# Linear attention beside an MLP on one core: the pass order of the key sums in six tiles, two relus and an operand split issued ahead of the values' products, and w2's first split issued behind a copy

## The chip, the cores and the metric

One core of a Trainium2 chip runs the whole kernel. The metric is the device time of one execution in microseconds. Of the kernel before there are three timed runs and one profiled execution, whose trace is read below.

The engines by their names in the trace: PE is TensorE (its matmuls), PEld its weight loads, DVE is VectorE, ACT is ScalarE, POOL is GpSimd, SP issues transfers. Each engine works through its own instructions in the order in which the program lists them, and waits for the others through semaphores. All times are in microseconds.

## The reference

The input is x (2048 tokens of 512 numbers), normalised to xn. Two branches read xn and their results are added to x:

```python
def attention(xn, wqkv, wo):                 # 32 heads of 16
    q, k, v = split_heads(xn @ wqkv)
    phi = lambda t: where(t > 0, t + 1, exp(t)) + 1e-6
    kv  = einsum("bhsd,bhse->bhde", phi(k), v)
    z   = einsum("bhsd->bhd", phi(k))
    num = einsum("bhqd,bhde->bhqe", phi(q), kv)
    den = einsum("bhqd,bhd->bhq", phi(q), z) + 1e-6
    return merge_heads(num / den) @ wo

def mlp(xn, w1, b1, w2, b2):                 # 512 -> 1376 -> 512
    r = relu(xn @ w1 + b1)
    return (r * r) @ w2 + b2

out = x + attention(layernorm(x), wqkv, wo) + mlp(layernorm(x), w1, b1, w2, b2)
```

## The kernel before

**Numbers in two parts.** Matmul operands are pairs of float32r tiles: a high part, which is the number rounded by a copy (mostly on ScalarE), and a low part, the number less its high part (a subtraction on VectorE or, for the tokens, on GpSimd). A product then is three matmuls: high by high, high by low, low by high. `split` (line 117) makes both parts.

**The order of work is written out by hand.** The program is recorded under a manual schedule: each engine gets its instructions in the order in which the Python code issues them, and semaphores are set by the tiles that the instructions share. Moving a line of Python therefore moves an instruction in the queue of its engine, and nothing else is rearranged.

**First stage: the tokens, tile by tile.** Sixteen tiles of 128 tokens are loaded, normalised and turned. The loop of line 778 runs over them. For tile i it projects the keys (`project`, line 367: twelve matmuls into a bank `pk`), makes phi of the keys (`phi`, line 359, on ScalarE and VectorE), then `parts` (line 373) gives phi's high part on ScalarE and its low part on VectorE (line 378), and `tokens` (line 349) makes the two parts of the normalised tokens of the next tile, the high part on ScalarE, the low part on GpSimd (line 119). Behind that, `kx` (line 384) adds tile i - 1 into four banks: the product of the tokens (turned) by phi(k). This is the key sum from which the attention's values are made later, since the weights of the values are applied after the sum. `kx` issues twelve matmuls in three groups of four. `tok[i][:, u]` with u = 0 or 1 is the high or low part of the tokens, `pk[i][:, v]` that of phi. For tiles 0 to 7 the groups come in the order (0,0), (0,1), (1,0): phi's low part is read by the second group, the tokens' low part by the third. Tiles 8 to 15 have an order of their own. A bank is done when all three groups are in, in whichever order.

**Work that is spread.** A list `extra` holds operand preparations for the next stage, each a small function; `more()` issues the next few of them at fixed places (the counts are written out on line 766).

**Between the stages** (lines 848 to 963, with n = 0). PE runs, in this order: `plain_1` into `pz` (twelve matmuls: the last, partly filled group of the MLP's hidden units, for the last 512 tokens), the last `kx`, `plain_1` into `pz2` (the same units for the 512 tokens before), and the values' products: `values()` (line 870) has 32 matmuls of 128 columns into a bank `pkv`; then VectorE masks the result to its heads (line 880, tile `kv`) and `split` makes its parts (tile `kvt`: the high part on ScalarE, the low part on VectorE). After `values()` one `more()` comes, then `relu` twice (line 475, ScalarE: the banks `pz` and `pz2` into `rz` and `r2[NF - 1]`, tiles `r2c`), then the remaining preparations of `extra`, then `piece_2(NF - 1, 0)` (line 196), which loads the last rows of w2 and returns two functions: one for the high part (ScalarE) with copies of it on GpSimd, and one for the low part (VectorE).

**Second stage** (line 1024). Queries and hidden units are made for two groups of 512 tokens at a time by a scheme that saves products: with weights and tokens cut into two halves each, seven products of six matmuls stand for eight. `product` (line 484) is one of them; its weights come from tiles `aop`, its tokens from the turned tokens `xs0`, `xs1` or from sums and differences `T[1]` to `T[4]`, and sums of weights are called S1 to S4. Every step p issues, with A, B and C as banks: A from A11; B from A12, adding c11, a copy of A in SBUF; C from S1 by T[1] and its copy t5; then more. In step 0 the small products `matrix(j)` (line 885, bank `pm`) stand between them; they read `kvt`. C's bank in step 0 is the one that held `pz`. `next_2(t)` (line 974) issues the functions that `piece_2` returned and asks for the next piece of w2; before the change it is called with 0 ahead of the loop, that is, ahead of step 0's products and copies, for both n. For n = 1 the list of pieces is empty at that point.

Accumulation of both branches, the residual and the store follow and are not touched.

Of the kernel before, what the change touches and what calls it, by code (L numbers as in the profile page):

```python
# [18 lines left out]
def kernel(  # L19
# [41 lines left out]
    NPE = 2 * TB  # L61
# [16 lines left out]
    def bank(name, tag="ps"):  # L78
        return psum.tile([P, 512], F32, name=name, tag=tag)

    def w512(name, tag, bufs):
        return work.tile([P, 512], F32, name=name, tag=tag, bufs=bufs)
# [26 lines left out]
    def copy(eng, o, i, bias=0.0):  # L109
        if eng == "act":  # L110
            nc.scalar.activation(o, i, AF.Copy, bias=bias)  # L111
        elif bias:
            ENG[eng].tensor_scalar(o, i, bias, None, op0=OP.add)
        else:
            ENG[eng].tensor_copy(o, i)

    def split(h, l, src, eh, el):
        copy(eh, h, src)
        ENG[el].tensor_tensor(out=l, in0=src, in1=f32(h), op=OP.subtract)  # L119
# [76 lines left out]
    def piece_2(f, at):  # L196

        h, l = w2s[f] = [w2r[at // 2][:, at % 2 * 2 + u] for u in range(2)]
        if f < NF - 1:
            t = raw(f"r2_{f}", w2[f * P:(f + 1) * P, :])  # L200
            return [lambda: copy("act", h, t), lambda: rest_of(l, t, h)]


        t = w512(f"r2_{f}", "raw", 6)
        for a, o, n in units(f):
            nc.sync.dma_start(t[a:a + n], w2[o:o + n, :])

        def high():
            copy("act", h, t)
            copy("pool", l[2 * Q:], h[:2 * Q])  # L210
            if "q" not in w2s:
                w2s["q"] = work.tile([P, D], F32R, name="w2q", tag="w2q")
                for k in range(TB):
                    copy("pool", w2s["q"][k * Q:(k + 1) * Q], h[2 * Q:3 * Q])

        def low():
            rest_of(l[:2 * Q], t[:2 * Q], h[:2 * Q])
            rest_of(h[3 * Q:], t[3 * Q:], h[3 * Q:])

        return [high, low]  # L220
# [161 lines left out]
        phi(ps, kp[i], mid, late)  # L382

    def kx(i):
        order = (((1, 0),), ((0, 0), (0, 1))) if i >= NPE else (((0, 0),), ((0, 1),), ((1, 0),))
        todo = [(c, u, v) for group in order for c in range(NJ) for u, v in group]
        first, last = order[0][0], order[-1][-1]
        for c, u, v in todo:
            nc.tensor.matmul(kxp[c], lhsT=tok[i][:, u, c * P:(c + 1) * P], rhs=pk[i][:, v],  # L389
                             start=i == 0 and (u, v) == first, stop=i == NT - 1 and (u, v) == last)  # L390
# [21 lines left out]
    def steps_of(t, j, done=False, parts=False):  # L412


        o = q[t][:, j]
        tiles = []
        blocks = lambda ap: ap.rearrange("p (r c) -> p r c", c=32)
        heads_of = lambda ap: ap.rearrange("p (h d) -> p h d", h=H)
        by_heads = lambda ap: ap.rearrange("p (r h) d -> p r h d", h=2)

        def weighted():
            pz = w512(f"pz{t}_{j}", "p", 6)
            tiles.append(pz)
            nc.scalar.activation(pz, o, AF.Identity, bias=zc[:, 1, j:j + 1], scale=zc[:, 0, j:j + 1])

        def sums():
            pt = w512(f"pt{t}_{j}", "p", 6)
            den = small.tile([P, H], F32, name=f"dt{t}_{j}", tag="den")
            nc.vector.transpose(blocks(pt), blocks(tiles[0]))
            nc.vector.tensor_reduce(den, heads_of(pt), axis=AX.X, op=OP.add)  # L430
            tiles.append(den)

        def quotients():
            pz, den = tiles
            nc.vector.tensor_scalar(den, den, 1e-6, None, op0=OP.add)
            nc.vector.reciprocal(den, den)
            nc.vector.transpose(by_heads(heads_of(pz)), by_heads(den[:, :, None].to_broadcast([P, H, D // H])))

        def divide():
            nc.vector.scalar_tensor_tensor(o, o, 1e-6, tiles[0], op0=OP.add, op1=OP.mult)  # L440

        def into_parts():
            a = aT[t, j] = places.pop(0)
            split(a[:, 0], a[:, 1], o, "act", "dve")

        return [lambda: phi_T(o, o)][done:] + [weighted, sums, quotients, divide] + [into_parts][:parts]
# [28 lines left out]
    def relu(o, i, f):  # L475
        nc.scalar.activation(o, i, AF.Relu, bias=b1s[:, f:f + 1])

    def plain_1(ps, w, x):

        for j in range(NJ):  # L480
            three(ps, [w[:, u, j * P:(j + 1) * P] for u in range(2)],
                  [x[u][:, j, :] for u in range(2)], j == 0, j == NJ - 1)

    def product(ps, a, b, first=False, last=False):

        for j in range(2):
            for n, (u, v) in enumerate(PASSES):
                nc.tensor.matmul(ps, lhsT=a[u][:, j * P:(j + 1) * P], rhs=b[v][:, j, :],  # L488
                                 start=first and j == 0 and n == 0, stop=last and j == 1 and n == 2,
                                 skip_group_check=True)  # L490
# [50 lines left out]
    for i0 in range(0, NT, TB):  # L541
# [5 lines left out]
        n = TB if i0 >= NPE else NPE - NDVE  # L547
        o = work.tile([P, n, 512], F32, name=f"xg{i0}", tag="r0" if i0 + TB == NT else "r3" if i0 >= NPE else "rc")
        for k in range(0, n, 2):
            i = i0 + TB - n + k  # L550
# [172 lines left out]
    def do(what, k=1):  # L723
        for _ in range(k):
            if what:
                what.pop(0)()
# [39 lines left out]
    extra, counts = [], [[0, 0, 0, 0, 0, 1, 1, 0, 0, 1, 2, 2, 0, 1, 4, 1, 2]]  # L766

    def more(i=None):

        if i is None or i > 12:  # L770
            do(extra, counts[0].pop(0))
# [3 lines left out]

    kxp = [bank(f"kx{c}", "acc") for c in range(NJ)]
    kx(0)
    for i in range(2, NT):
        if i == 3:
# [60 lines left out]
        if i in (3, 6):  # L840

            b = i // 6
            for u in range(2):
                nc.sync.dma_start(xsd[b][u], f32(cols(b * TB)[u]))
        kx(i - 1)
        more(i)

# [4 lines left out]
    plain_1(pz, z, xlast[0])  # L852
    more()
    kx(NT - 1)
    kxs = [two(f"kxs{c}") for c in range(2)]
    for c in range(NJ):
# [13 lines left out]
    def values():  # L870
        ps = bank("pkv", "acc")
        for c in range(NJ):
            for j in range(NJ):
                at = slice(j * P, (j + 1) * P)

                nc.tensor.matmul(ps[:, at], lhsT=wvs[:, c, at], rhs=kxs[c // 2][:, c % 2, at],  # L876
                                 start=c == 0 and j == 0, stop=c == NJ - 1 and j == NJ - 1,
                                 skip_group_check=True)
        t = w512("kv", "p", 6)
        nc.vector.tensor_tensor(out=t.rearrange("p (j d) -> p j d", j=NJ), in0=ps.rearrange("p (j d) -> p j d", j=NJ),  # L880
                                in1=heads[:, None, :].to_broadcast([P, NJ, P]), op=OP.mult)
        kvt[0] = work.tile([P, 2, 512], F32R, name="kvt", tag="r3")
        split(kvt[0][:, 0], kvt[0][:, 1], t, "act", "dve")
# [16 lines left out]
    for n in range(2):  # L900
# [4 lines left out]
        order = [("q", 0), ("w", 0), ("q", 1), *(("w", k) for k in range(1, NP))]  # L905
# [37 lines left out]
        if n == 0:  # L943

            more()
            pz2 = bank("pz0b")
            plain_1(pz2, z, x2)
            more()
            values()
            more()  # L950

            rz = r2[1]
            relu(rz, pz, NF - 1)
            relu(r2[NF - 1], pz2, NF - 1)
            do(extra, len(extra))
            w2next = piece_2(NF - 1, 0)
        else:
            w2next = []
            pz = bank(f"pz{n}", "acc")
            plain_1(pz, z, x1)  # L960
# [13 lines left out]
        def next_2(t):  # L974

            do(w2next, 2 - highs.pop(0))
            if t + 1 < NF and (n == 0 or t >= TB - 1):
                f = w2order[t + 1]
                w2next.extend(piece_2(f, place(f)))

        def high_2():
            do(w2next)
            highs[0] = 1

        highs = [0] * NF
        next_2(0)


        banks = [bank(f"b{n}_{k}") for k in range(4)]
# [29 lines left out]
        def step(k=1):  # L1019

            for _ in range(k):
                do(steps[t1] or steps[t2])

        for p in range(NO + 1):
# [24 lines left out]
            if kind:  # L1049
                c11 = w512(f"c11_{n}_{p}", "p", 6)  # L1050
                copy("act", c11, A)
                product(B, A12, [x[:, 2:] for x in x1], True, True)
                if kind == "w":
                    high_2()
                nc.vector.tensor_tensor(out=c11 if kind == "w" else q[t1][:, fa], in0=B, in1=c11, op=OP.add)
                if kind == "w":
                    relu(c11, c11, fa)
                else:
                    steps[t1] += steps_of(t1, fa, parts=True)
                step(at_p[0])  # L1060
# [261 lines left out]
```

## Time and profile before

| | us |
|---|---|
| median of 3 timed runs | 415.05 (414.95 to 415.22) |
| the profiled execution | 415.3 |
| its span, first to last instruction | 413.6 |
| PE busy | 408.6 |
| PEld busy | 336.9 |
| DVE busy | 314.5 |
| ACT busy | 270.2 |
| POOL busy | 50.0 |

The span is what the trace shows; the time of the execution has 1.7 around it. PE's busy time is modelled from pipelined matmuls, so a busy PE may still be waiting between two of them; the weight loads show the waits, and the chain of waits, which follows the work that ended last back through the program, shows how long each run of matmuls really took. A row of the timeline gives start, length, engine, line, operation, the tile that is written and those that are read, their sizes, a count, and in brackets how long the engine stood idle before it and what it then waited for. A line of the source can be that of a helper: line 111 is every copy on ScalarE, line 119 every subtraction in `split`.

### The profile page before, as it was taken

Reading aid. Unit: us, or ns where it says so; the run is one execution under the profiler, and the core shown is the slowest. Engines: PE = TensorE matmul, PEld = TensorE weight load, DVE = VectorE, ACT = ScalarE, POOL = GpSimd, SP = SyncE. Lnnn points to the kernel's source line nnn. Section 1 sums busy time; section 2 is a strip of 40 time slices with the busy share of each in tenths; the row PEclk is TensorE's granted clock in tenths of the full one; section 3 lists DMA queues with packets and bytes.
Section 4 is the critical chain, followed back from the end, with each engine's and each line's share of the span. In section 5 each row is a group of like instructions: output and inputs, shape, how many; then the busy total and the mean of one; then the engine's idle time right before and its main releaser. Section 6 shows DMA issues by size and latency. Waiting matters only on the chain.

```text
span 413.6 us, 5427 instructions
## 1 busy us (share of the span) xinstructions
PE 408.6 (99%) x1835; PEld 336.9 (81%) x1835; DVE 314.5 (76%) x584; ACT 270.2 (65%) x487; POOL 50.0 (12%) x70
## 2 busy tenths in 40 slices
PE   8999999999999999999999999999999999999996
PEld 7788888888888888888878888888888888878885
DVE  6895667797699898998439996468989685449843
ACT  5867767756668888789547731567588857737420
POOL 3241222230130000020000040100000200000310
PEclk9999999999999999999999999999999999999999
DMA  7789572710321312264267991411120871025602
GB/s 248 272 247 353 204 228 101 234 48 2 102 77 52 101 41 72 93 177 78 89 246 251 385 198 75 129 52 48 54 79 25 228 183 47 2 86 168 103 0 101
DMA packets 44925, 54.62 MB, mean 132 GB/s; under 512 B 7905, under 2 KB 29153, under 8 KB 43618
## 3 DMA queue, kind: packets, MB, share of 16 engines
q1 hardware_dynamic: 42594, 50.09, 37.1%
q0 software_dynamic: 2304, 4.20, 6.5%
q8 instruction: 14, 0.23, 0.2%
q14 instruction: 13, 0.11, 0.1%
HBM read 41.16 MB, written 13.11 MB: 131 GB/s over the span
## 4 chain that ended last, share of the span: by engine, by line
PE 97%; DMA 1%; ACT 0%; SPq 0%; DVE 0%; issue 0%
PE acc L130 37%; PE b L488 32%; PE kx L389 11%; PE pk L370 11%; PE acc L499 2%; PE pz L130 1%; DMA rk<-in_A_wqkv_dram 1%; PE pkv L876 1%; PE pm L130 1%; PE pz0b L130 1%; PE b L130 1%; PE pt L309 1%; PE acc L506 0%; SPq L159 0%; PE end L130 0%; ACT wkh L111 0%
## 5 line engine op out<-in xcount | busy, mean ns | idle before, releaser
L130 PE MATMUL acc<-w2r,s 128*128 128x512 f32 x477 | 112.9, 390 | 0.0
L130 PEld LDWEIGHTS acc<-w2r,s 128*128 128x128 f32 x477 | 89.4, 188 | 19.3 <-issue 0.7
L488 PE MATMUL b<-T,aop 128*128 128x512 f32 x336 | 83.9, 390 | 0.0
L488 PEld LDWEIGHTS b<-T,aop 128*128 128x128 f32 x336 | 62.8, 188 | 13.9 <-DVE aop L119 0.4
L389 PE MATMUL kx<-pk,tok 128*128 128x512 f32 x192 | 46.8, 392 | 0.0
L389 PEld LDWEIGHTS kx<-pk,tok 128*128 128x128 f32 x192 | 35.6, 188 | 8.0 <-DVE pk L378 0.6
L488 PE MATMUL b<-xs0h,aop 128*128 128x512 f32 x112 | 36.9, 390 | 0.0
L1005 POOL DMA_DIRECT2D res<-in_B_b_dram x16 | 14.1, 1099 | 182.4 <-DVE dt L430 64.1
L130 PE MATMUL acc<-mh,aTsr 128*128 128x512 f32 x112 | 35.6, 389 | 0.0
L119 POOL TENSOR_TENSOR tok<-xp,tok 128x512 fp32r<-128x512 f32 x16 | 22.3, 1393 | 55.1 <-ACT tok L111 55.1
L1013 DVE TENSOR_TENSOR res<-acc,res 128x512 f32<-128x512 f32 x16 | 11.0, 692 | 23.1 <-PE acc L130 18.5
L122 DVE TENSOR_TENSOR w2r<-r,w2r 128x512 fp32r<-128x512 f32 (+2 forms) x35 | 25.2, 721 | 0.1
L111 ACT ACTIVATE aop<-S 128x512 fp32r<-128x512 f32 x28 | 17.5, 624 | 11.1 <-DVE S L705 11.1
L130 PEld LDWEIGHTS acc<-mh,aTsr 128*128 128x128 f32 x112 | 21.0, 188 | 4.4
L488 PEld LDWEIGHTS b<-xs0h,aop 128*128 128x128 f32 x112 | 21.0, 188 | 4.3
L119 DVE TENSOR_TENSOR aop<-S,aop 128x512 fp32r<-128x512 f32 x28 | 19.5, 697 | 4.3 <-ACT aop L111 3.9
L119 DVE TENSOR_TENSOR s<-c,s 128x512 fp32r<-128x512 f32 x20 | 13.6, 689 | 11.0 <-ACT s L111 11.0
L130 PE MATMUL acc<-ml,aTsr 128*128 128x512 f32 x56 | 21.8, 389 | 0.0
L488 PE MATMUL b<-xs0l,aop 128*128 128x512 f32 x56 | 21.8, 389 | 0.0
L111 ACT ACTIVATE w2r<-r 128x512 fp32r<-128x512 f32 x32 | 19.6, 619 | 2.6 <-DMA out_dram<-res 2.0
L111 ACT ACTIVATE T<-Tf 128x512 fp32r<-128x512 f32 x16 | 9.5, 628 | 16.5 <-DVE Tf L648 16.4
L488 PE MATMUL b<-xs1h,aop 128*128 128x512 f32 x56 | 19.5, 389 | 0.0
(197 smaller groups left out, 770.0 us busy)
## 6 DMA issues: line engine op xcount, KB each, us to landing
r<-in_B_w_dram SPq DMA_DIRECT2D x49, 256.0 KB, 3.0
res<-in_A_x_dram SPq DMA_DIRECT2D x8, 512.0 KB, 4.7
res<-in_B_b_dram POOLq DMA_DIRECT2D x16, 256.0 KB, 5.7
out_dram<-res SPq DMA_DIRECT2D x15, 256.0 KB, 2.1
x<-in_A_x_dram SPq DMA_DIRECT2D x5, 512.0 KB, 5.8
via<-xp SPq DMA_DIRECT2D x5, 512.0 KB, 2.7
xg<-via SPq DMA_DIRECT2D x20, 128.0 KB, 2.9
xTd<-t SPq DMA_DIRECT2D x8, 256.0 KB, 3.4
```

The costliest lines, as they stand in the source:

```text
L111: nc.scalar.activation(o, i, AF.Copy, bias=bias)
L119: ENG[el].tensor_tensor(out=l, in0=src, in1=f32(h), op=OP.subtract)
L122: nc.vector.tensor_tensor(out=l, in0=src, in1=f32(h), op=OP.subtract)
L130: nc.tensor.matmul(ps, lhsT=a[u], rhs=b[v], start=first and n == 0, stop=last and n == 2)
L309: nc.tensor.transpose(t[k][:, at:at + P], xp[i][:, j * P:(j + 1) * P], ident)
L370: nc.tensor.matmul(ps, lhsT=cols(i)[u][:, j, slot(i)], rhs=w[v][:, j, :], start=first and n == 0, stop=last and n == len(steps) - 1)
L389: nc.tensor.matmul(kxp[c], lhsT=tok[i][:, u, c * P:(c + 1) * P], rhs=pk[i][:, v], start=i == 0 and (u, v) == first, stop=i == NT - 1 and ( ...
L488: nc.tensor.matmul(ps, lhsT=a[u][:, j * P:(j + 1) * P], rhs=b[v][:, j, :], start=first and j == 0 and n == 0, stop=last and j == 1 and n == 2,
L499: nc.tensor.matmul(ps, lhsT=s[u][:, k * P:(k + 1) * P], rhs=w2s[NF - 1][u][:, a:z], start=first and u == 0, stop=stop and u == 1)
L876: nc.tensor.matmul(ps[:, at], lhsT=wvs[:, c, at], rhs=kxs[c // 2][:, c % 2, at], start=c == 0 and j == 0, stop=c == NJ - 1 and j == NJ - 1 ...
L1005: nc.gpsimd.dma_start(r[:, i], b2[None, :].partition_broadcast(P), accum_op=OP.add)
L1013: nc.vector.tensor_tensor(out=r[:, a:z], in0=ps, in1=r[:, a:z], op=OP.add)
```

## The change

Three edits. In `kx`, tiles 2 to 7 get the order (0,0), (1,0), (0,1): the tokens' low part is read by the second group and phi's low part by the last; tiles 0 and 1 keep the old order, and so do 8 to 15. Between the stages the two relus and the next two entries of `extra` are issued ahead of `values()` instead of behind it, and the two `more()` around `values()` go; every entry of `extra` is still issued, once. The call `next_2(0)` ahead of the loop stays for n = 1; for n = 0 it moves into step 0, behind the copy c11.

```diff
     def kx(i):
-        order = (((1, 0),), ((0, 0), (0, 1))) if i >= NPE else (((0, 0),), ((0, 1),), ((1, 0),))
+        if i >= NPE:
+            order = ((1, 0),), ((0, 0), (0, 1))
+        elif i > 1:
+            order = ((0, 0),), ((1, 0),), ((0, 1),)
+        else:
+            order = ((0, 0),), ((0, 1),), ((1, 0),)
...
             pz2 = bank("pz0b")
             plain_1(pz2, z, x2)
             more()
-            values()
-            more()
 
             rz = r2[1]
             relu(rz, pz, NF - 1)
             relu(r2[NF - 1], pz2, NF - 1)
+            do(extra, 2)
+            values()
             do(extra, len(extra))
             w2next = piece_2(NF - 1, 0)
...
         highs = [0] * NF
-        next_2(0)
+        if n:
+            next_2(0)
...
                 c11 = w512(f"c11_{n}_{p}", "p", 6)
                 copy("act", c11, A)
+                if n == 0 and p == 0:
+                    next_2(0)
                 product(B, A12, [x[:, 2:] for x in x1], True, True)
```

Engine by engine, the program holds the same instructions in both versions. On PE only the two groups in `kx` of tiles 2 to 7 trade places, and the first and the third `pm` matmul now carry waits for `kvt`. ScalarE's order around the values' products was kvt, S1, relu, relu, part of A22, S3, w2, c11, t5; it is relu, relu, S1, kvt, the part of A22, S3, c11, w2, t5. VectorE's was kv, kvt, T[1]'s low part, S1's low part, T[2]'s; it is T[1]'s, S1's, kv, kvt, T[2]'s. The transfers and GpSimd's copies keep their order; the load of the next piece of w2 waits, before and after, for S1's low part, whose data held its buffer.

## The prediction

> **What bounds the kernel now.** I read the page first, then the waits of the weight loader (the half of TensorE where its waits show), then the chain of waits, then the timeline around each place where the chain takes longer than its matmuls need.
>
> ```profile
> span 413.6 us, 5427 instructions
> ...
> PE 97%; DMA 1%; ACT 0%; SPq 0%; DVE 0%; issue 0%
> ```
>
> The matrix engine is on the chain for 97% of the span, and the diff neither adds nor removes a matmul. So the change can only win what TensorE still waits, and only lose by making it wait anew. All of its waits that bear on the edits:
>
> ```profile
> PEld kx L389 <- DVE pk L378: 0.6, 2, 0.3
> PEld b L488 <- DVE aop L119: 0.4, 1, 0.4
> PEld b L488 <- ACT r2c L476: 0.3, 1, 0.3
> PEld b L488 <- DVE t L1037: 0.2, 1, 0.2
> ```
>
> These are idle times of the loader, part of which the matmul in flight hides. The chain (start, duration, what) shows what is really lost:
>
> ```profile
> 20.14 2.98 PE kx L389 x12
> ...
> 26.29 2.75 PE kx L389 x12
> ...
> 32.21 2.77 PE kx L389 x12
> ...
> 37.70 2.72 PE kx L389 x12
> ...
> 106.56 4.58 PE b L488 x18
> 111.14 1.39 PE pm L130 x6
> ...
> 125.26 9.64 PE b L488 x42
> ```
>
> Twelve undisturbed matmuls take 2.72, so one takes 0.227. Then 18 need 4.08 and lost 0.50 at 106.56; 42 need 9.52 and lost 0.12 at 125.26.
>
> **Part 1, the order of kx for tiles 2 to 7.** It swaps the second and third groups of four matmuls: tokens' low part with phi's high part now comes second, phi's low part third. The two waits for phi's low part (0.3 each) belong to tiles 0 and 1: their kx is the one that starts before 26 (the second is the 2.98 row), and these keep the old order. Tiles 4 to 7 run at 2.72 already, tiles 2 and 3 at 2.75 and 2.77 with no wait named. So at most 0.03 + 0.05 = 0.08 could be won. What can be lost: the tokens' low part is subtracted by GpSimd and is wanted four matmuls sooner. For tile 2 that is close:
>
> ```profile
> 24.69 1.96 POOL L119 TENSOR_TENSOR tok<-xp,tok 128x512 fp32r<-128x512 f32 x1 [4.25 <-ACT tok L111]
> ...
> L119 POOL TENSOR_TENSOR tok<-xp,tok 128x512 fp32r<-128x512 f32 x8 | 11.1, 1398 | 25.8 <-ACT tok L111 25.8
> ...
> 26.83 0.19 PEld L389 LDWEIGHTS kx<-pk,tok 128*128 128x128 f32 x1
> ```
>
> The subtraction ends at 24.69 + 1.96 = 26.65, and the fifth weight load of tile 2, which the new order feeds from it, starts at 26.83: 0.18 to spare. From tile 3 on the tokens are made a whole tile ahead: all eight subtractions of tiles 2 to 9 take 11.1, so the seven others 1.31 each, and tile 3's, next in the queue, is done near 28.0, four before its kx at 32.21. Nothing ahead of 26.83 is edited, so I take 0, with bounds of -0.08 and, should this subtraction last one more DVE instruction (0.69, as in the DVE rows below), 0.69 - 0.18 = +0.51.
>
> **Part 2, two relus and a split ahead of the values' products.** The lost 0.50 lies here:
>
> ```profile
> 108.94 0.39 PE L488 MATMUL b<-xs0h,aop 128*128 128x512 f32 x1
> 109.24 0.30 PEld L488 LDWEIGHTS b<-T,aop 128*128 128x128 f32 x2 [0.34 <-ACT r2c L476]
> 109.93 0.76 PEld L488 LDWEIGHTS b<-T,aop 128*128 128x128 f32 x4 [0.40 <-DVE aop L119]
> 110.97 0.40 PE L130 MATMUL pm<-wo,kvt 128*128 128x512 f32 x1
> ```
>
> The row at 108.94 is the last of twelve matmuls of A11 and A12. Undisturbed, the next six (S1 by T1) would start at 108.94 + 0.23 = 109.17 and the pm product behind them at 109.17 + 1.36 = 110.53. It starts at 110.97: 0.44 is lost, first to the relu that frees the bank, then to S1's low part. The rest, 0.06, is the change over from the values' products, which stays. Why both are late, on ScalarE and VectorE:
>
> ```profile
> 102.71 0.61 ACT L111 ACTIVATE aop<-rq 128x512 fp32r<-128x512 f32 x1
> 107.32 0.63 ACT L111 ACTIVATE kvt<-kv 128x512 fp32r<-128x512 f32 x1 [4.00 <-DVE kv L880]
> 107.86 0.61 ACT L111 ACTIVATE aop<-S 128x512 fp32r<-128x512 f32 x1
> 108.50 0.69 ACT L476 ACTIVATE r2c<-pz,b1s 128x512 f32<-128x512 f32 x1
> 109.08 0.68 ACT L476 ACTIVATE r2c<-pz0b,b1s 128x512 f32<-128x512 f32 x1
> ...
> 110.48 0.63 ACT L111 ACTIVATE w2r<-r 128x512 fp32r<-128x512 f32 x1
> 111.00 0.60 ACT L111 ACTIVATE c<-b 128x512 f32<-128x512 f32 x1
> ...
> 113.95 0.67 ACT L111 ACTIVATE aop<-r 128x512 fp32r<-128x512 f32 x1
> ```
> ```profile
> 103.35 0.69 DVE L119 TENSOR_TENSOR aop<-rq,aop 128x512 fp32r<-128x512 f32 x1 [1.65 <-ACT aop L111]
> 106.59 0.69 DVE L880 TENSOR_TENSOR kv<-pkv,heads 128x512 f32<-128x512 f32 x1 [2.55 <-PE pkv L876]
> 107.98 0.69 DVE L119 TENSOR_TENSOR kvt<-kv,kvt 128x512 fp32r<-128x512 f32 x1 [0.70 <-ACT kvt L111]
> 108.59 0.68 DVE L122 TENSOR_TENSOR T<-Tf,T 128x512 fp32r<-128x512 f32 x1
> 109.19 0.69 DVE L119 TENSOR_TENSOR aop<-S,aop 128x512 fp32r<-128x512 f32 x1
> ```
>
> ScalarE stands 4.00 before kvt, because kvt waits for kv, and kv for the values' products; the split of S1 and the relus queue behind it though they need nothing of it. VectorE stands 2.55 before kv in the same way. In the new order ScalarE goes relu, relu, S1, kvt. Stepping as these rows do (0.64 after a copy, 0.57 after a relu), the relus start at 103.3 and 103.9, S1 at 104.5, done by 105.1; VectorE does T1's low part at 104.0 and S1's from 105.1 to 105.8. That is 1.8 of ScalarE's 4.00 and ends 0.8 before kv can start at 106.59, so kv, kvt's high part (107.32) and kvt's low part (to 108.67) stay where they are. What TensorE wants at 109.17 is ready at 105.8. The pm products now carry waits of their own for kvt; they want it at 110.53, 1.86 after it is done. This part: -0.44, with bounds 0 and -0.50. Were the cover gone (products of the values ending over 0.8 sooner), kvt would be late by what is lacking, against 1.86 to spare.
>
> **Part 3, w2's split behind c11's copy.** Three instructions now stand ahead of kvt, so what follows it moves up by that much: the two aop copies at 107.9 and 108.2, c11 at 108.7, the w2 copy at 109.2 (1.3 sooner than 110.48, though one place further back). Behind it in ScalarE's queue are t5, T3's two copies and m's; in VectorE's the rests of w2, then T3's low parts; on GpSimd the five casts. If w2's data were late all of these would wait. It is loaded by the first of these:
>
> ```profile
> 104.77 1.61 SPq L206 DMA_DIRECT2D r<-in_B_w_dram  x3
> ...
> 109.91 0.35 SPq L165 DMA_DIRECT2D r<-in_B_w_dram  x1
> ...
> r<-in_B_w_dram SPq DMA_DIRECT2D x5, 256.0 KB, 2.9
> ```
>
> The last of the three is issued by 106.4; with 2.9 to landing that is 109.3 at worst, 0.1 after the copy could start, and t5 cannot start before its product ends near 110.7. The transfer at 109.91 waited for S1's low part, which held its buffer; it moves up to about 107.4, behind the loads of the next weights, whose data is first copied at 113.95 (the last of ScalarE's rows), by then near 113.4. So part 3 itself costs 0; bounds: -0.03 (the pm row's 1.39 for 1.36) and +0.1.
>
> **The second loss, 0.12 at 125.26,** is a bank held until VectorE's addition of line 1037. By the windows (length; PE, weight loads, DVE, ACT, POOL busy) VectorE has hardly a gap up to there:
>
> ```profile
> 112.40:126.00 13.60, 13.60 (x61) 11.25 (x60) 13.43 (x24) 10.39 (x21) 4.72 (x6) 1.00 0.21 62
> ```
>
> With 1.2 taken out of its front (T1, S1: 108.59 to 109.80) and TensorE 0.44 ahead, the addition gains on TensorE by more than the 0.12. I take -0.10, bounds 0 and -0.12.
>
> **The sum:** 0 - 0.44 + 0 - 0.10 = -0.54; span 413.06. The profiled execution took 415.3, 1.7 more than its span, and 0.25 more than the median of 415.05. On the median: **414.5**. The bounds give 415.05 - 0.08 - 0.50 - 0.03 - 0.12 = 414.3 to 415.05 + 0.51 + 0.1 = 415.7, if every cost fell at its worst and nothing were won.
>
> **The rivals.** *Taken back later (415.05).* TensorE, 0.44 ahead, meets something that did not move, and waits there. For it: VectorE's 13.43 of 13.60. Against: VectorE, ScalarE and two transfers move up by more than TensorE does, and no later wait of TensorE for another engine is named.
>
> *Collision with GpSimd (414.85).* The casts start 1.3 sooner, beside other subtractions.
>
> ```profile
> 112.55 3.64 POOL L115 CAST w2q<-w2r 32x512 fp32r<-32x512 f32 x4
> 113.67 2.04 DVE L122 TENSOR_TENSOR T<-Tf,T 128x512 fp32r<-128x512 f32 x2
> 119.66 1.28 DVE L122 TENSOR_TENSOR T<-Tf,T 128x512 fp32r<-128x512 f32 x2
> ```
>
> Beside the casts two subtractions of T3 took 2.04; alone, those of T4 take 1.28. T3's second low part should now come near 114.5. Behind pm (110.53), T2's six, pm's three, six of xs1 and three more, T3's own product starts 24 matmuls later, at 115.97, and its fifth wants that part at 116.88. If each of the four subtractions from w2's rests on waits for a whole cast (3.64 / 4 = 0.91), that is 3.64 against 0.76 paid already: 2.9 later, at 117.4, 0.5 late: 415.05 - 0.44 + 0.5 = 415.1. Half as much costs only the second gain, 414.6. I enter the middle.
>
> By the Trainium skill (SBUF — State Buffer, section "SBUF: two separate sides") VectorE and GpSimd take a shared pair of ports by an exclusive lock for a whole instruction, and the loser fully blocks. The trace agrees in kind, 2.04 beside 1.28; taken at its fullest the rule gives the 415.1, while the gap in time measured here leaves the forecast as it is.
>
> *Slower: tile 2's tokens come late (415.3).* Place: the fifth weight load of kx of tile 2. It decides once the subtraction ends after 26.83 + 0.54 = 27.37, when it costs more than the rest wins. The others take 1.31, this one 1.96, so it has been held up by about one VectorE instruction (0.69) already. Held up by one more it ends at 27.34 and the time is 415.0; by two more, at 28.03, 1.20 late: 415.05 - 0.54 + 1.20 = 415.7. Between the two: 415.3. Against: nothing ahead of it on any engine is changed.
>
> *No gain at all from kx's order* is part of my forecast, not a rival.
>
> **How the numbers follow.** Forecast 0.68 (its own range 414.3 to 414.75, by the bounds of parts 2 and the second loss and 0.15 for the spread of the runs shown), taken back 0.16, collision 0.08, slower 0.03; 0.05 for more than the bounds. The range 414.15 to 415.15 leaves out the slower case and part of the last. What a measurement can tell from no change here is about 0.2%, 0.83. Faster by that means under 414.22, the low edge of the forecast and the last case: 0.12. Slower by that, over 415.88: 0.03. Within: 0.85.
>
> **What would show it.** In the new profile the relus stand near 103.3 and S1's copy before kvt; the 18 matmuls at 106.56 take about 4.14, and the two waits of 0.3 and 0.4 are gone; kvt's subtraction still ends near 108.7; the 42 matmuls near 124.8 take 9.52; kx of tile 2 takes 2.75 or less. I am wrong if kx of tile 2 shows a wait for GpSimd, if pm waits for kvt, or if a new wait between 111 and 135 holds 0.3 or more.

## The result and the profile after

| | before | changed |
|---|---|---|
| median of 21 runs each, side by side | 415.11 | 414.44 |
| ratio, 95% interval | | 0.9984 (0.9978 to 0.999) |
| span of the profiled execution | 413.6 | 412.9 |

The change makes the kernel faster by 0.16%, 0.67 in the medians and 0.7 in the span; the forecast was 0.54. That is less than the 0.2% that the prediction took as the least that a measurement can tell from no change; with 21 runs on each side the interval still excludes 1. One correction to the description of the change: of the two calls of `more()` around `values()`, only the one behind it goes.

The waits of the weight loads that belong to the engines' work, of the changed kernel:

```profile
PEld pk L370 <- ACT xs1h L325: 0.7, 2, 0.5
PEld kx L394 <- DVE pk L378: 0.6, 2, 0.3
PEld kx L394 <- ACT pk L111: 0.2, 1, 0.2
```

All three waits of line 488 before (for a relu, for S1's low part, for the addition) are gone; the two for phi's low part are unchanged. The chain of waits of the changed kernel (start, duration, what) says what that was worth:

```profile
16.73 2.92 PE kx L394 x12
...
20.09 2.98 PE kx L394 x12
...
26.24 2.75 PE kx L394 x12
...
32.16 2.77 PE kx L394 x12
...
102.94 3.57 PE pkv L881 x32
106.51 4.13 PE b L493 x18
110.64 1.37 PE pm L130 x6
...
124.75 9.52 PE b L493 x42
...
136.99 9.52 PE b L493 x42
```

18 matmuls take 4.13 instead of 4.58, the six of pm 1.37 for 1.39, the 42 take 9.52 for 9.64: 0.59. The four kx rows (tiles 0 to 3) are what they were, to the hundredth. For what follows, a yardstick helps that leaves out the start of the execution: the path from the values' products (`pkv`) to the second run of 42. It is 136.99 - 102.94 = 34.05; before it was 137.64 - 102.98 = 34.66. That 0.61 is nearly all of the change; the other 0.1 of the span lies in a first kx that starts 0.05 sooner and in what follows the second 42.

ScalarE and VectorE of the changed kernel, from the timeline:

```profile
103.29 0.69 ACT L481 ACTIVATE r2c<-pz,b1s 128x512 f32<-128x512 f32 x1
103.88 0.68 ACT L481 ACTIVATE r2c<-pz0b,b1s 128x512 f32<-128x512 f32 x1
104.45 0.63 ACT L111 ACTIVATE aop<-S 128x512 fp32r<-128x512 f32 x1
107.27 0.63 ACT L111 ACTIVATE kvt<-kv 128x512 fp32r<-128x512 f32 x1 [2.19 <-DVE kv L885]
...
108.64 0.58 ACT L111 ACTIVATE c<-b 128x512 f32<-128x512 f32 x1
109.12 0.62 ACT L111 ACTIVATE w2r<-r 128x512 fp32r<-128x512 f32 x1
```
```profile
105.11 0.69 DVE L119 TENSOR_TENSOR aop<-S,aop 128x512 fp32r<-128x512 f32 x1 [0.52 <-ACT aop L111]
...
107.93 0.69 DVE L119 TENSOR_TENSOR kvt<-kv,kvt 128x512 fp32r<-128x512 f32 x1 [0.70 <-ACT kvt L111]
```

The relus and S1 now stand inside ScalarE's wait for kv, which shrinks from 4.00 to 2.19 and ends where it ended. S1's low part is done at 105.8, and TensorE asks for it without a pause:

```profile
108.89 1.32 PEld L493 LDWEIGHTS b<-T,aop 128*128 128x128 f32 x6
110.25 1.33 PEld L130 LDWEIGHTS pm<-wo,kvt 128*128 128x128 f32 x6
```

### The profile page after: what moved, and what is told of

Same layout as the page of the kernel before. It is cut to its first block, busy times and chain, and to the rows that moved or that the text cites. A ratio compares the mean times of both kernels' runs of the same rounds, so it can differ in the third digit from the quotient of the medians.

```text
span 412.9 us, 5426 instructions
## 1 busy us (share of the span) xinstructions
PE 407.9 (99%) x1835; PEld 337.1 (82%) x1835; DVE 314.6 (76%) x584; ACT 270.3 (65%) x487; POOL 49.7 (12%) x70
## 4 chain that ended last, share of the span: by engine, by line
PE 98%; DVE 1%; DMA 1%; ACT 0%; issue 0%
PE acc L130 37%; PE b L493 32%; PE kx L394 11%; PE pk L370 11%; PE acc L504 2%; PE pz L130 1%; PE pkv L881 1%; PE pm L130 1%; PE pz0b L130 1%; PE b L130 1%; DMA x<-in_A_x_dram 1%; PE pt L309 1%; DVE st L230 0%; PE acc L511 0%; PE end L130 0%; DVE xp L269 0%
```

## The experiments

The path named in each is that yardstick: 34.66 before, 34.05 in the changed kernel. It is read from one execution each, but it varies little: the changed kernel, its second execution and the five variants of it below all have 34.05. The medians are of 11 or 12 runs beside at least 23 of the kernel before.

**One edit at a time.** The order of kx alone, on the kernel before:

```diff
-        order = (((1, 0),), ((0, 0), (0, 1))) if i >= NPE else (((0, 0),), ((0, 1),), ((1, 0),))
+        if i >= NPE:
+            order = ((1, 0),), ((0, 0), (0, 1))
+        elif i > 1:
+            order = ((0, 0),), ((1, 0),), ((0, 1),)
+        else:
+            order = ((0, 0),), ((0, 1),), ((1, 0),)
```

> The kernel before with the new group order of kx for tiles 2 to 7 alone. Theory (this edit is worth nothing, since none of these tiles waited): time as before within 0.1 us, kx of tiles 2 and 3 at 2.75 and 2.77 in the chain, the 18 matmuls behind the values' products still at 4.58, the 42 at 9.64. Rival (the order gives part of the 0.67 us that the median fell): the kx rows of tiles 2 to 7 get shorter together by 0.1 us or more and the time falls by as much. Rival (tile 2's tokens come late): kx of tile 2 over 2.85, with a wait for GpSimd.

Measured: 415.22 beside 415.21, ratio 1.0002 (0.9992 to 1.0012). Tiles 2 and 3 stand at 2.77 and 2.76, and the path is 34.65. From the chain of this kernel:

```profile
106.46 4.57 PE b L493 x18
...
125.25 9.57 PE b L493 x42
```

The first loss is there in full. The second shows 0.05 here instead of 0.12, but the path as a whole is as long as before. The edit is worth nothing.

The two preparations ahead of the values' products, the relus left behind them, on the kernel before:

```diff
-            values()
-            more()
+            do(extra, 2)
+            values()
```

> The kernel before with only the two preparations (T[1]'s low part and the split of S1) ahead of the values' products; the relus stay behind them, w2's split ahead of c11. Theory (the wait that ends last is S1's low part on VectorE; the relus, one split sooner, end near 108.6 and free the bank before it is wanted at 108.94): nearly all of the gain is here, the 18 matmuls at 4.13 to 4.20, the 42 at 9.52, time 0.5 to 0.65 us under before. Rival (both waits count, and each edit gives about half): the 18 matmuls near 4.35 and a wait for the relu of 0.2 or more.

Measured: 414.85 beside 415.21, ratio 0.9993 (0.9984 to 1.0001). The chain of this kernel:

```profile
103.26 3.57 PE pkv L876 x32
106.83 4.13 PE b L488 x18
...
125.07 9.56 PE b L488 x42
...
137.37 9.52 PE b L488 x42
```

The first loss is gone by this edit alone, and no weight load waits for a relu. The path is 34.11: 0.55 of the 0.61. The medians show less, 0.36; the interval holds that, 0.55 and no gain at all, so the size rests on the chain.

The two relus alone, on the kernel before:

```diff
-            values()
-            more()
-
             rz = r2[1]
             relu(rz, pz, NF - 1)
             relu(r2[NF - 1], pz2, NF - 1)
+            values()
+            more()
```

> The kernel before with only the two relus ahead of the values' products. Theory (S1's low part ends last and stands where it stood): the wait for the relu goes, the one for S1's low part stays and takes its place; 18 matmuls still at 4.5 to 4.6, 42 at 9.64 or a little less, time as before within 0.1 us. Rival (both waits count, each edit gives about half): 18 matmuls near 4.35, time 0.2 us or more under before.

Measured: 415.30, ratio 1.0004 (0.9995 to 1.0012), path 138.09 - 103.38 = 34.71. The wait of the weight loads, and the chain of this kernel:

```profile
PEld b L488 <- DVE aop L119: 0.6, 1, 0.6
```
```profile
106.99 0.70 DVE kv L880
107.69 0.02 issue
107.72 0.64 ACT kvt L111
108.36 0.02 issue
108.38 0.69 DVE kvt L119
109.07 0.60 DVE T L122
109.67 0.61 DVE aop L119
```

The wait for the relu is gone and the one for S1's low part has grown from 0.4 to 0.6: it ends last, and takes over what the other gave up. Here the chain (the rows follow one another without a gap) leaves TensorE and shows the cause by name: S1's low part stood behind kv, kvt and T[1] on VectorE.

w2's split behind c11 alone, on the kernel before:

```diff
-        next_2(0)
+        if n:
+            next_2(0)
...
                 copy("act", c11, A)
+                if n == 0 and p == 0:
+                    next_2(0)
```

> The kernel before with only w2's first split behind c11's copy. Theory (worth nothing by itself: c11 comes 0.5 us sooner and the split 0.5 us later, and neither was waited for): time as before within 0.1 us, 18 matmuls at 4.58, pm's six at 1.37 to 1.39. Rival (c11's copy or t5 held the products behind pm): pm's and the next product's rows fall by 0.03 us or more. Rival (the split was wanted): a new wait behind 120, time 0.1 us or more over before.

Measured: 415.50, ratio 1.0012 (1.0003 to 1.002), path 137.87 - 102.93 = 34.94. The theory as written for this run is wrong: alone, the edit costs 0.28. From the waits, the chain and VectorE's timeline of this kernel:

```profile
PEld b L488 <- DVE t L1038: 0.4, 1, 0.4
...
PEld b L488 <- ACT sz L111: 0.2, 1, 0.2
```
```profile
125.40 9.75 PE b L488 x42
```
```profile
111.57 1.71 DVE L122 TENSOR_TENSOR w2r<-r,w2r 64x512 fp32r<-64x512 f32 x2 [0.21 <-ACT w2r L111]
...
121.10 0.68 DVE L1038 TENSOR_TENSOR q<-b,t 128x512 f32<-128x512 f32 x1
```

The w2 copy, one place later on ScalarE, makes VectorE stand 0.21 before w2's rests (its low part). They start 0.89 behind the instruction ahead of them (110.68 to 111.57); in the kernel before it was 0.61 (110.73 to 111.34), so VectorE is 0.28 late. It hardly stands still behind that, so what follows on it comes late, and TensorE meets it in two places. One is the addition of the second loss (line 1037 before, 1038 here; 0.4 instead of 0.2), at 133. The other is the same product one step sooner, at 121.89, where no other kernel here has a named wait. The list puts that one down to sz, a copy on ScalarE that ended at 121.69; but by the program the product does not read sz. It goes on in a bank that the addition at 121.10 has to read first, and that ended later, at 121.78; so I take the wait to be for the addition, which is argued from the program and not shown by the list. So it does matter to TensorE when w2's split is done, by way of VectorE's queue.

**The same edit in the company of the others:** the changed kernel with w2's split back ahead of the loop.

```diff
-        if n:
-            next_2(0)
+        next_2(0)
...
-                if n == 0 and p == 0:
-                    next_2(0)
```

> The changed kernel with w2's first split back ahead of the loop, as before the change. Theory (VectorE binds, and w2's rests start there near 110.1 whichever of the two copies ScalarE does first, since both are done by 109.8): same as the changed kernel within 0.1, no new wait of TensorE. Rival (the third edit is needed: with the split ahead c11 is late): a wait of 0.1 or more at the products behind pm. Rival (the third edit costs here what it costs alone): 0.2 to 0.3 under the changed kernel.

Measured: 414.72 beside 415.28, ratio 0.9991 (0.998 to 1.0002); path 137.11 - 103.06 = 34.05, no wait of line 493. The interval holds both 1 and the ratio of the changed kernel, so this too rests on the chain. With the relus and S1 out of the way both copies are done (by 109.86) before VectorE can take w2's rests (at 110.21), and which is first does not matter.

**The margin at tile 2.** The changed kernel, with the tokens' low part in tile 2's first group:

```diff
-        elif i > 1:
+        elif i == 2:
+            order = ((1, 0),), ((0, 0),), ((0, 1),)
+        elif i > 1:
```

> The changed kernel with the tokens' low part read by the first group of tile 2, four matmuls sooner still. Theory (the margin at tile 2 is 0.2 in front of the second group, and TensorE pays each microsecond beyond it): the subtraction ends near 26.6, the first weight load would come at 25.97, so kx of tile 2 takes 2.75 plus 0.6 and the time is 0.55 to 0.65 over the changed kernel. Rival (slack behind takes it up): the wait shows, but less than 0.3 of it in the time.

Measured: 415.39 beside 415.28, ratio 1.0009 (1.0001 to 1.0018), where the changed kernel has 0.9984; span 413.6, where the changed kernel has 412.9. The weight loads and the chain of this kernel:

```profile
PEld kx L396 <- POOL tok L119: 0.7, 1, 0.7
```
```profile
24.74 1.96 POOL tok L119
26.69 0.04 issue
26.74 3.01 PE kx L396 x12
```

The subtraction of GpSimd is on the chain, and the whole gain of the change is gone: 0.7 in the span, 0.7 in that wait, a little more than the 0.55 to 0.65 expected. The lateness at this place was paid in full. In the change itself the margin held:

```profile
24.64 1.95 POOL L119 TENSOR_TENSOR tok<-xp,tok 128x512 fp32r<-128x512 f32 x1 [4.25 <-ACT tok L111]
...
26.78 0.19 PEld L394 LDWEIGHTS kx<-pk,tok 128*128 128x128 f32 x1
```

These are rows of the changed kernel: 26.59 against 26.78, 0.19 to spare.

**Where the waits for phi's low part are.** The change leaves out tiles 0 and 1, the two that wait. The new order for these too:

```diff
-        elif i > 1:
-            order = ((0, 0),), ((1, 0),), ((0, 1),)
-        else:
-            order = ((0, 0),), ((0, 1),), ((1, 0),)
+        else:
+            order = ((0, 0),), ((1, 0),), ((0, 1),)
```

> The changed kernel with the new group order of kx for tiles 0 and 1 too. Theory (each wait is judged by what is late next): tile 0 gains nothing, since tile 1's kx behind it waits anyway for phi's high part from ScalarE (done near 19.9); tile 1's 2.98 falls to 2.72, 0.26 won; but tile 2's fifth weight load then comes at 26.5 and its tokens' low part ends near 26.6, so 0.05 to 0.1 is given back there with a wait for GpSimd. Net 0.15 to 0.25 under the changed kernel. Rival (waits add up freely): both rows fall to 2.72 and the time by 0.46. Rival (no room): nothing, a new wait eats it all.

Measured: 414.59 beside 415.28, ratio 0.9986 (0.9975 to 0.9997). From the waits, the chain and the timeline of this kernel:

```profile
PEld kx L392 <- ACT pk L111: 0.4, 2, 0.2
```
```profile
16.87 2.77 PE kx L392 x12
...
20.07 3.01 PE kx L392 x12
...
26.25 2.79 PE kx L392 x12
```
```profile
20.07 2.59 PEld L392 LDWEIGHTS kx<-pk,tok 128*128 128x128 f32 x12 [0.23 <-ACT pk L111]
```

Both waits for VectorE are gone. Tile 0, which was expected to win nothing, wins 0.15; tile 1, which was expected to win 0.26, is reached sooner and stays at 3.01, since it now waits for phi's high part in front instead of for the low part inside. So the theory had the two tiles the wrong way round. From the first kx to the values' products it is 102.95 - 16.87 = 86.08 for 86.21 in the changed kernel: 0.13 is won, a little less than the least expected. Nothing is given back at tile 2: from its start to the values' products it takes 76.70 in both kernels. The timed runs do not show the gain; the ratio is no lower than the changed kernel's 0.9984.

The new order for tile 1 alone, the old for tiles 0 and 2 to 7:

```diff
-        elif i > 1:
+        elif i == 1:
```

> The changed kernel with the new group order of kx for tile 1 alone; tiles 0 and 2 to 7 in the old order. Theory: tile 1's 2.98 falls to 2.72 and nothing is given back at tile 2, whose phi low part is done at 25.5: 0.26 under the changed kernel, no wait of the weight loads for GpSimd, one instead of two waits for phi's low part. Rival (what follows tile 1 is late anyway): the row falls, but the next projection or tile 2's kx waits for it, net under 0.1.

Measured: 414.60 beside 415.28, ratio 0.9982 (0.9973 to 0.999). The chain, and the timeline of ScalarE and of the weight loads, of this kernel:

```profile
20.22 2.86 PE kx L394 x12
```
```profile
19.36 0.63 ACT L111 ACTIVATE pk<-k 128x512 fp32r<-128x512 f32 x1 [0.24 <-DVE k L365]
...
20.05 2.61 PEld L394 LDWEIGHTS kx<-pk,tok 128*128 128x128 f32 x12
```

Tile 1 falls to 2.86, not to 2.72: phi's high part is done at 19.99, and the first weight load of tile 1 starts 0.06 behind it, at 20.05. In the run before, where the list does name that wait, it started 0.05 behind it, and in the changed kernel 0.05 too. So the 2.98 held two losses in a row, one to each engine, and the order can only win the second. To see whether the gain is real, the changed kernel and this one were timed once more side by side.

> The changed kernel itself, for a comparison side by side with the next one. 0.55 to 0.75 us under before; from the first kx to the values' products 86.2, from there to the first pm product 7.70.

> The changed kernel with tile 1's kx in the new order and tiles 2 to 7 in the old, a second time. In the trace of its first execution tile 1 took 2.86 and the way from the first kx to the values' products 86.05 instead of 86.21. Theory: the same again, 0.1 to 0.2 us under the changed kernel. Rival (that was the spread of one execution): 86.2 and no difference of the medians beyond 0.1.

Measured: 414.66 for the changed kernel and 414.46 for this one, beside 415.50 before; the ratios are 0.998 (0.9971 to 0.999) and 0.998 (0.9969 to 0.999). From the first kx to the values' products the two executions took 86.14 and 86.06. The chain has the gain in all executions on record: with the new order in tile 1 or in both tiles it is 86.05 to 86.08 (three executions), with the old order 86.14 to 86.24 (eight, the kernel before and the single edits among them). The intervals of the timed runs do not part the two kernels. So a version that may be better by 0.1 is at hand, and is not shown to be.

## Why the prediction was right

*The bound.* Only TensorE's own waits could be won. The rows that moved are the two that were shown with a loss, and the list of the changed kernel names no new wait.

*Part 1, 0 for the order of kx.* Shown by the single edit (ratio 1.0002), and by rows that stayed the same. The worry beside it was real: the margin was 0.19, and in the experiment on tile 2 a wait of 0.7 at this place cost 0.7.

*Part 2, -0.44.* The rows give -0.45 and another -0.02 at pm. The steps were as written, to within 0.05 at the relus, S1 and its low part, and kvt stood where it had stood. What the prediction did not say is that the two moves are not equal: it had the loss "first to the relu that frees the bank, then to S1's low part". The single edits show that the two preparations alone make up the first loss, and that the relus give nothing without them. With S1 moved, the relus come early enough for the bank where they were. What the relus add then is small, 0.06 of the path (34.11 to 34.05), and it comes by another way, told at the second loss below.

*Part 3, 0.* Right for this change, as the run with the split back ahead shows. But its bound of +0.1 holds only beside part 2: alone, the edit costs 0.28, nearly three times that. The prediction did name VectorE's rests of w2 as what waits for this copy, but looked only at whether w2's data would be late. That the copy's own place in ScalarE's queue can make them late, on an engine that has hardly a gap, was left out there and in the expectation for the single edit.

*The second loss, -0.10.* It went in full, -0.12. That it hangs on when VectorE's addition ends can be read from the traces. The product that waits for it has six matmuls of 0.227 ahead of it in the same stretch of weight loads, so its first load would come 1.36 behind the start of that stretch. That time, and the end of the addition, from the timelines:

| kernel | addition ends | product asks for the bank | addition late by | the 42 take |
|---|---|---|---|---|
| w2's split alone | 133.44 | 133.17 | 0.27 | 9.75 |
| before | 133.20 | 133.04 | 0.16 | 9.64 |
| order of kx alone | 133.10 | 133.02 | 0.08 | 9.57 |
| the two preparations alone | 132.84 | 132.85 | -0.01 | 9.56 |
| changed | 132.10 | 132.52 | -0.42 | 9.52 |

The later the addition, the longer the 42. The prediction had the addition gain on TensorE by more than 0.12; it gained 0.58. The addition in the kernel before and in the changed one:

```profile
132.52 0.68 DVE L1037 TENSOR_TENSOR t<-b,t 128x512 f32<-128x512 f32 x1
```
```profile
131.42 0.68 DVE L1043 TENSOR_TENSOR t<-b,t 128x512 f32<-128x512 f32 x1
```

The table also shows what the relus add. With the two preparations alone the addition ends only just in time. There the relus still stand behind kvt on ScalarE, and a copy behind them makes VectorE stand 0.30:

```profile
109.86 0.42 DVE L119 TENSOR_TENSOR aop<-rq,aop 128x256 fp32r<-128x256 f32 x1 [0.30 <-ACT aop L111]
```

With the relus moved too, that wait is gone.

*The sum.* -0.54 forecast, -0.67 measured in the medians. Of the difference, 0.02 is the second loss taken at -0.10, and 0.03 lies in the first loss and pm's row. The rest is 0.05 at the start and some hundredths behind the 42, which the forecast did not contain; the start is within what executions differ by (the first kx starts anywhere from 16.69 to 17.17 in the kernels above).

*The rivals.* Nothing was taken back later. The casts did start sooner, and the collision came along, at its old price:

```profile
111.29 3.64 POOL L115 CAST w2q<-w2r 32x512 fp32r<-32x512 f32 x4
```
```profile
112.42 2.04 DVE L122 TENSOR_TENSOR T<-Tf,T 128x512 fp32r<-128x512 f32 x2
```

In these rows of the changed kernel the casts take 3.64 and T3's subtractions 2.04, as before, 1.25 sooner. The case in which each of the four subtractions waits for a whole cast did not occur. Tile 2's tokens were in time.

## What to carry to other kernels

In queues that run in order, put what is ready ahead of what waits: a wait of 4.00 on ScalarE cost nothing by itself, but a split queued behind it was wanted by the busiest engine. Of two waits in a row, the one that ended last held nearly the whole gain here, and single edits told which that was better than the list of waits did. An edit that is free in the company of others can cost by itself: judge it by what it releases on an engine that has no gap, and not only by who reads its result.

## What the runs showed that was not expected

VectorE sets TensorE's pace far into the second stage of the kernel before, though it is busy for 76% of the span: being 0.28 late at 111.57 came out as 0.28 of time, at two places 10 and 22 us later. And one wait can hide another inside the same run of matmuls: tile 1's kx took 2.98, 0.26 over the undisturbed 2.72, with one wait named in the list at 0.3. When that wait went, the row gave up only 0.12. The other 0.14 I put down to the wait in front, for phi's high part, which the list of that run does not name.
